# Downward products five units behind the upward ones instead of four

## The chip, the core and the metric

The kernel runs on one core of one Trainium2 chip. The metric is the device time of one execution in microseconds (us), lower is better. The engines go by the profile's names: PE is TensorE's matmul stream and PEld its weight loads, DVE is VectorE, ACT ScalarE, POOL GpSimd, and SP is SyncE, which here only issues DMAs.

## What is computed

Four batches of 12608 tokens with 128 channels go through an attention with 32 inducing points, and its output through a channel mix with a hidden width of 1024:

```python
h = mab(I, x)                  # 32 inducing points attend to all tokens
x = mab(x, h)                  # every token attends to the 32 results
xk = mu_k * x + (1 - mu_k) * x_prev      # x_prev: the token before
xr = mu_r * x + (1 - mu_r) * x_prev
k = np.maximum(xk @ w_k, 0.0)            # 128 -> 1024, "upward"
v = k * k @ w_v                          # 1024 -> 128, "downward"
r = 1.0 / (1.0 + np.exp(-(xr @ w_r)))    # the gate
out = r * v
```

## The kernel before

Each batch is cut into 25 groups of 512 tokens (the last has 320), and each group into four units of 256 of the 1024 hidden channels, so there are 100 units in a batch and 400 in all. A table `units` lists them, and one loop runs over them with the step number `n`; `u` is the place of the unit in its group, 0 to 3. The schedule is written out by hand: every engine carries out its instructions in the order in which this loop emits them, and waits by semaphores for what they need.

Step `n` emits, in this order:

- `gate` (L816, DVE), in the step after a group's last downward product: the output in the PSUM bank `ps_v` times the gate `rT`.
- `up(n)` (L780, L782, PE): four matmuls of 512 columns into one of two `ps_a` tiles. They read `R`, the attention's weights of this group's tokens, and `W`, the hidden layer's weights folded with the inducing points' values.
- `square(n)`: DVE takes the maximum with zero out of `ps_a` into `k_t` (L792; called relu below). ACT squares it into `kh`, rounded to the matmul's format (L797), and into `k_t` (L798). POOL forms the rest `kl`, the difference of the two (L800). In two steps of twelve (`high_vector`) DVE makes `kh` instead of ACT (L794), and ACT's L798 then waits for it.
- `zgate` (L769, L770 on PE; L772 on ACT) in one step of four, `u == 1`: two matmuls into the group's `ps_v` bank and the sigmoid from there to `rT`. The downward products later write over the same bank, so the first of them waits for the sigmoid.
- `store` (L827, DVE; L834, SP), one step after `gate`: a transpose, and after every second group four DMAs of 128 KB to the output.
- `down(n - LAG)` (L811, PE): six matmuls, `kh` by two weight tiles and `kl` by one.
- the `events` of step `n`: the attention of later tokens, cut into small pieces with a step number each.

Of these events three matter here. `stage_a` prepares the next batch: `btr` (L331, DVE, then four DMAs `xt<-xs`, L334) transposes tokens at steps s-1, s, s+1 and s+3 of each twelve, through three `xs` buffers. `stage_b` makes `R`: its softmax pieces run on DVE and ACT, its last DVE piece is `al` (L661), and `spread` (L594, L671) one step later issues five DMAs a group on SP, one of them the halo of one column from the group before, for four groups in four steps. SP issues its DMAs strictly in the emitted order.

`kh` and `kl` have as many buffers as the distance `LAG`, so `kh` of unit n goes where that of unit n - LAG was, and waits for the downward product that step n emits. `k_t` has four buffers, `ps_a` and `ps_v` two each.

Before the loop a head reads batch 0, runs its first attention and converts the weights; it borrows the buffers of `kh` and `kl` (`halves`).

Of the kernel before, what the change touches and what calls it, by code (L numbers as in the profile page):

```python
# [8 lines left out]
F32 = mybir.dt.float32  # L9
F32R = mybir.dt.float32r  # L10
# [9 lines left out]
def kernel(  # L20
# [11 lines left out]
    nc = tc.nc  # L32
# [3 lines left out]
    P = 128  # L36
    Q = 4
    FC = F // P
    G = 512
# [2 lines left out]
    TAIL = N - (NBLK - 1) * BLK  # L42
    WF = F + C
    UC = 2
    LAG = 4
    UO = 2
    NU = FC // UC
    assert NBLK == 7 and C == P and M * Q == P and F % 1024 == 0 and TAIL % Q == 0
# [9 lines left out]
    mp = ctx.enter_context(tc.tile_pool(name="mp", bufs=2))  # L58
# [530 lines left out]
    def halo(S, g, far=True):  # L589

        if g == 0:
            nc.vector.memset(S.R[g].bitcast(F32)[:, 0:1], 0.0)
        elif far:
            nc.sync.dma_start(out=S.R[g].bitcast(F32)[:, 0:1], in_=S.R[g - 1].bitcast(F32)[:, G:G + 1])  # L594
        else:
            nc.vector.tensor_copy(out=S.R[g][:, 0:1], in_=S.R[g - 1].bitcast(F32)[:, G:G + 1])
# [157 lines left out]
    class Group:  # L754
# [31 lines left out]
        def square(self, u, on_vector):  # L786

            w = self.w
            k = mp.tile([P, UC * G], F32, name="k_t", bufs=4).rearrange("p (c t) -> p c t", c=UC)[:, :, :w]
            kh = mp.tile([P, UC, G], F32R, name="kh", bufs=4)[:, :, :w]  # L790
            kl = mp.tile([P, UC, G], F32R, name="kl", bufs=4)[:, :, :w]
            nc.vector.tensor_scalar(out=k, in0=self.ps[:, :, :w], scalar1=0.0, scalar2=None, op0=ALU.max)  # L792
            if on_vector:
                nc.vector.scalar_tensor_tensor(out=kh, in0=self.ps[:, :, :w], scalar=0.0, in1=k,  # L794
                                               op0=ALU.max, op1=ALU.mult)
            else:
                nc.scalar.activation(out=kh, in_=k, func=AF.Square)  # L797
            nc.scalar.activation(out=k, in_=k, func=AF.Square)  # L798
            self.h[u] = (kh, kl)
            return lambda eng, a, z: eng.tensor_tensor(out=kl[:, :, a:z], in0=k[:, :, a:z],  # L800
                                                       in1=kh.bitcast(F32)[:, :, a:z], op=ALU.subtract)
# [36 lines left out]
    def run(th):  # L838
        for f in th:
            f()  # L840
# [6 lines left out]
    def halves():  # L847

        for name in ("kh", "kl"):
            for _ in range(4):  # L850
                yield mp.tile([P, UC, G], F32, name=name, bufs=4)

    pairs = halves()

    conv = {}
# [43 lines left out]
    def head():  # L899


        last = NBLK - 1
        for k in range(2):
            ab[k].tr()
        place(PARTS_FIRST)
        ab[0].scores()
        for k in range(NBLK):
            ab[k].maxi()
            ab[k].expo()
            place(PARTS[k][0])  # L910
            if k > 0:
                ab[k - 1].hmm()
            if k == last:
                maxes()
            if k > 0:
                ab[k - 1].acc()
            if k == 0:
                constants()
            if k + 2 < NBLK:
                ab[k + 2].tr()  # L920
            place(PARTS[k][1])
            ab[k].etrans()
            ab[k].ecopy()
            ab[k].sums()
            if k < last:
                ab[k + 1].scores()
            place(PARTS[k][2])
        spin(8)
        weights()
        ab[last].hmm()  # L930
        ab[last].acc()
        load_x(1, 0)
        hfin()
        assert not work
# [11 lines left out]
    def start():  # L946

        sc0, df0, ex0, nm0, pl0 = stage_b_head([0, 1])
        sc1, df1, ex1, nm1, pl1 = stage_b_head([2, 3])
        hi0, lo0, put0 = pl0[0]  # L950
        box = {}

        def bank():
            return pv.tile([P, G], F32, name="ps_v")

        def gate_bank(s):
            if s == 0:
                box["g"] = bank()
            return box["g"][:, s * C:(s + 1) * C]

        wa = [wpart(s, 0, bank) for s in range(2)]
        wb = [wpart(s, 1, bank) for s in range(2)]
        wg = [wpart(s, None, lambda s=s: gate_bank(s)) for s in range(2)]
        assert F // G == 2
        hi1, lo1, put1 = pl0[1]
        run([sc0, lambda: halo(batches[0], 0), df0, wa[0][0], wa[1][0], wa[0][1], ex0, wa[1][1], wa[0][2], nm0, wb[0][0], hi0, lo0, put0,
             wa[1][2], wb[0][1], hi1, lo1, wb[0][2]])
        for f in (wb[1][0], wb[1][1]):
            soon(0, f)
        for n, f in ((0, wb[1][2]), (0, sc1), (1, df1), (1, ex1), (2, nm1)):  # L970
            at(n, f)
        for prod, high, low in wg:
            at(1, prod)
        for prod, high, low in wg:
            at(1, high)
            at(2, low)
        soon(2, put1)
        for k, (high, low, put) in enumerate(pl1):
            at(k + 2, high)
            at(k + 3, low)  # L980
            at(k + 5, put)
        at(4, lambda: units[0][0].zgate(first=True))
# [22 lines left out]
    with tc.manual_schedule():  # L1005
        head()
        start()
        for n in range(len(units) + LAG + 2):
            grp, u = units[n] if n < len(units) else (None, n % NU)
            old, ou = units[n - LAG] if LAG <= n < len(units) + LAG else (None, 0)  # L1010
            m = n - LAG - 1
            if 0 <= m < len(units) and units[m][1] == NU - 1:
                units[m][0].gate()
            if grp is None:
                run(late)
                late = []
            else:
                grp.up(u)
                run(early.pop(n, []))
                low = grp.square(u, n in high_vector)  # L1020
                run(late)
                late = []
                part = grp.w - (grp.w // 2 if n >= len(units) - 3 else 0)
                low(nc.gpsimd, 0, part)
                if part < grp.w:
                    late = [lambda low=low, a=part, z=grp.w: low(nc.vector, a, z)]
                if n == end:
                    run(late)
                    late = []
                if n >= NU and u == 1:  # L1030
                    grp.zgate()
                if u == NU - 2 and n + 2 < len(units):
                    nxt = units[n + 2][0]
                    if nxt.b == 0 and nxt.g < Q:
                        halo(nxt.S, nxt.g, far=False)
            if 1 <= m <= len(units) and units[m - 1][1] == NU - 1:
                units[m - 1][0].store()
            if old is not None:
                old.down(ou)
            run(events.pop(n, []))  # L1040
# [30 lines left out]
```

## Time and profile before

| | |
|---|---|
| median of 3 runs | 1141.57 us (1140.73 to 1146.31) |
| profiled execution, first to last instruction | 1141.9 us |
| its own time | not given apart; its span is 0.3 us above the median |
| busy PE, PEld | 1100.8, 836.7 us |
| busy DVE, ACT, POOL | 917.5, 971.6, 948.5 us |
| POOL `kl` (L800), 400 times | 2.377 us each |
| DVE relu (L792), 400 times | 1.201 us each |
| ACT squares (L797, L798) | 1.040 and 1.049 us each |
| the loop's first upward product | at 58.26 us |

PE's busy time counts overlapped matmuls with modelled ends, so a short pause hides in it; the waits that the profile puts down to a releaser are the better guide. Idle time of another engine costs nothing unless PE waits for it in the end.

### The profile page before, as it was taken

What the parts mean: (1) busy time and instruction counts of PE and PEld (TensorE: products, weight loads), DVE (VectorE), ACT (ScalarE), POOL (GpSimd) and SP (SyncE); (2) the same over time, 40 slices, a digit from 0 to 9 for tenths busy, and PEclk for the clock granted to TensorE, in tenths of its full rate; (3) what the DMA queues carried; (4) which work ended last, traced back from release to release, by engine and by line L of the source; (5) the groups of instructions that cost most, each with busy time, mean ns of one, the idle gap of its engine ahead of it and who ended that gap; (6) DMA issues with size and microseconds to landing.
All of it is one profiled execution on the core that took longest, in us unless ns stands there. A gap on an engine that the chain in (4) does not pass through costs nothing.

```text
span 1141.9 us, 17672 instructions
## 1 busy us (share of the span) xinstructions
PE 1100.8 (96%) x5710; PEld 836.7 (73%) x5710; DVE 917.5 (80%) x1294; ACT 971.6 (85%) x1107; POOL 948.5 (83%) x413
## 2 busy tenths in 40 slices
PE   6788999999989999999999999999999999999997
PEld 4466777777777777777777777777778777777886
DVE  4787899887678988887777889898777888887665
ACT  4487888888988888888987988889889988889996
POOL 1157888988877988888889888888888899999996
PEclk9989999999999999999999999999999999999999
DMA  9213454555135455555134455545222233242212
GB/s 268 75 29 92 106 111 108 127 129 106 33 67 119 94 124 123 125 120 124 23 63 86 110 127 121 131 96 125 49 51 60 45 65 59 54 74 56 43 28 34
DMA packets 274988, 102.32 MB, mean 90 GB/s; under 512 B 234288, under 2 KB 249808, under 8 KB 272592
## 3 DMA queue, kind: packets, MB, share of 16 engines
q1 hardware_dynamic: 274560, 101.18, 40.8%
q8 instruction: 45, 0.74, 0.3%
q14 instruction: 47, 0.39, 0.1%
q10 hardware_dynamic: 336, 0.02, 0.0%
HBM read 28.07 MB, written 25.82 MB: 47 GB/s over the span
## 4 chain that ended last, share of the span: by engine, by line
PE 80%; DVE 9%; ACT 7%; issue 3%; DMA 1%; SPq 0%; DVEq 0%; ACTq 0%
PE ps_v L811 40%; PE ps_a L780 15%; PE ps_a L782 13%; DVE k_t L792 3%; PE pb_b L617 2%; PE ps_v L769 2%; PE ps_v L770 2%; PE pb_a L359 2%; PE pb_a L428 2%; ACT kh L797 2%; ACT L772 1%; ACT L634 1%; ACT k_t L798 1%; DVE kh L794 1%; PE ps_a L227 1%
## 5 line engine op out<-in xcount | busy, mean ns | idle before, releaser
L800 POOL TENSOR_TENSOR kl<-k_t,kh 128x1024 fp32r<-128x1024 f32 (+2 forms) x400 | 939.6, 2377 | 151.7 <-ACT k_t L798 131.2
L792 DVE TENSOR_SCALAR k_t<-ps_a 128x1024 f32<-128x1024 f32 (+1 forms) x400 | 480.4, 1201 | 153.9 <-PE ps_a L782 144.2
L798 ACT ACTIVATE k_t<-k_t 128x1024 f32<-128x1024 f32 (+1 forms) x400 | 418.6, 1049 | 38.6 <-DVE kh L794 22.2
L797 ACT ACTIVATE kh<-k_t 128x1024 fp32r<-128x1024 f32 (+1 forms) x352 | 366.1, 1040 | 89.5 <-PE ps_v L811 49.8
L780 PE MATMUL ps_a<-R,W 128*128 128x512 f32 (+1 forms) x800 | 325.2, 407 | 8.8 <-DMA R<-al 4.7
L782 PE MATMUL ps_a<-R,W 128*128 128x512 f32 (+1 forms) x800 | 314.7, 394 | 0.0
L811 PE MATMUL ps_v<-kh,wvh 128*128 128x512 f32 (+1 forms) x800 | 250.2, 394 | 5.3 <-ACT rT L772 4.7
L811 PE MATMUL ps_v<-kl,wvh 128*128 128x512 f32 (+1 forms) x800 | 249.1, 392 | 0.2 <-POOL kl L800 0.2
L811 PE MATMUL ps_v<-kh,wvl 128*128 128x512 f32 (+1 forms) x800 | 249.2, 392 | 0.0
L780 PEld LDWEIGHTS ps_a<-R,W 128*128 128x128 f32 x800 | 151.7, 190 | 82.9 <-issue 20.0
L811 PEld LDWEIGHTS ps_v<-kh,wvh 128*128 128x128 f32 x800 | 149.7, 189 | 44.0 <-ACT rT L772 9.9
L811 PEld LDWEIGHTS ps_v<-kl,wvh 128*128 128x128 f32 x800 | 150.3, 189 | 34.8 <-POOL kl L800 0.4
L811 PEld LDWEIGHTS ps_v<-kh,wvl 128*128 128x128 f32 x800 | 150.6, 189 | 34.2
L782 PEld LDWEIGHTS ps_a<-R,W 128*128 128x128 f32 x800 | 151.7, 190 | 30.8
L816 DVE TENSOR_TENSOR oT<-ps_v,rT 128x512 f32<-128x512 f32 (+1 forms) x100 | 66.7, 667 | 2.3
L827 DVE STREAM_TRANSPOSE ot<-oT 128x512 f32<-128x512 f32 x96 | 67.3, 701 | 0.0
L794 DVE SCALAR_TENSOR_TENSOR kh<-ps_a,k_t 128x1024 fp32r<-128x1024 f32 x48 | 58.8, 1225 | 5.4 <-DVE k_t L792 0.5
L772 ACT ACTIVATE rT<-ps_v 128x512 f32<-128x512 f32 (+1 forms) x99 | 57.3, 579 | 0.3
L331 DVE STREAM_TRANSPOSE xs<-xb 128x512 f32<-128x512 f32 x72 | 50.0, 695 | 3.6 <-DMA xt<-xs 1.8
L769 PE MATMUL ps_v<-R,W 128*128 128x512 f32 (+1 forms) x99 | 39.1, 395 | 1.4 <-DVE oT L816 1.4
L772 ACT ACT_TABLE_LOAD x31 | 39.8, 1283 | 0.5
L770 PE MATMUL ps_v<-R,W 128*128 128x512 f32 (+1 forms) x99 | 38.7, 391 | 0.0
(192 smaller groups left out, 609.5 us busy)
## 6 DMA issues: line engine op xcount, KB each, us to landing
out_dram<-ot SPq DMA_DIRECT2D x184, 128.0 KB, 3.3
xb<-in_x_dram SPq DMA_DIRECT2D x18, 1024.0 KB, 5.5
xt<-xs SPq DMA_DIRECT2D x288, 64.0 KB, 2.0
R<-ah SPq DMA_DIRECT2D x184, 64.0 KB, 2.0
R<-al SPq DMA_DIRECT2D x184, 64.0 KB, 2.0
kh<-in_x_dram SPq DMA_DIRECT2D x4, 512.0 KB, 7.9
kl<-in_x_dram SPq DMA_DIRECT2D x4, 512.0 KB, 7.5
xb<-in_x_dram SPq DMA_DIRECT2D x8, 256.0 KB, 5.3
```

What stands on the lines that cost most here:

```text
L769: nc.tensor.matmul(out=ps[:, :w], lhsT=S.W[0][:, F:WF], rhs=R[:, 1:w + 1], start=True, stop=False)
L772: nc.scalar.activation(out=self.rT, in_=ps[:, :w], func=AF.Sigmoid)
L780: nc.tensor.matmul(out=ps[:, c, :w], lhsT=S.W[0][:, cs], rhs=R[:, 1:w + 1], start=True, stop=False)
L782: nc.tensor.matmul(out=ps[:, c, :w], lhsT=S.W[1][:, cs], rhs=R[:, 0:w], start=False, stop=True)
L792: nc.vector.tensor_scalar(out=k, in0=self.ps[:, :, :w], scalar1=0.0, scalar2=None, op0=ALU.max)
L794: nc.vector.scalar_tensor_tensor(out=kh, in0=self.ps[:, :, :w], scalar=0.0, in1=k, op0=ALU.max, op1=ALU.mult)
L797: nc.scalar.activation(out=kh, in_=k, func=AF.Square)
L798: nc.scalar.activation(out=k, in_=k, func=AF.Square)
L800: return lambda eng, a, z: eng.tensor_tensor(out=kl[:, :, a:z], in0=k[:, :, a:z], in1=kh.bitcast(F32)[:, :, a:z], op=ALU.subtract)
L811: nc.tensor.matmul(out=self.v, lhsT=wt[:, fc, :], rhs=kk[:, c, :], start=(fc == 0 and n == 0), stop=(fc == FC - 1 and n == 2))
L816: nc.vector.tensor_tensor(out=self.oT, in0=self.v, in1=self.rT, op=ALU.mult)
L827: nc.vector.transpose(out=ot[:, o:o + w], in_=self.oT)
```

## The change

The distance becomes five units, with five buffers each for `kh` and `kl`. Since a group then ends one step later, `gate` and `store` move by themselves from `u` = 0 and 1 to `u` = 1 and 2 (they are emitted by the distance), and `zgate` is moved from `u == 1` to `u == 2` by its condition. The events keep their step numbers. The two additional buffers take 8 KB of each partition, and an argument of the program's set-up gives up part of the memory that is reserved there for DMA descriptors.

```diff
-    LAG = 4
+    LAG = 5
...
-            kh = mp.tile([P, UC, G], F32R, name="kh", bufs=4)[:, :, :w]
-            kl = mp.tile([P, UC, G], F32R, name="kl", bufs=4)[:, :, :w]
+            kh = mp.tile([P, UC, G], F32R, name="kh", bufs=LAG)[:, :, :w]
+            kl = mp.tile([P, UC, G], F32R, name="kl", bufs=LAG)[:, :, :w]
...
-                yield mp.tile([P, UC, G], F32, name=name, bufs=4)
+                yield mp.tile([P, UC, G], F32, name=name, bufs=LAG)
...
-                if n >= NU and u == 1:
+                if n >= NU and u == LAG % NU + 1:
                     grp.zgate()
...
-    nc = _bacc.Bacc("TRN2", target_bir_lowering=False, num_devices=1)
+    nc = _bacc.Bacc("TRN2", target_bir_lowering=False, num_devices=1,
+                     dynamic_dma_scratch_size=1024)
```

What this does to the order is shown at three places. The numbers behind names tell tiles apart, and they differ between the two programs.

On PE, at the loop's start, the rows from the end of `up(4)` on. Before:

```order
L782 MATMUL ps_a_861<-R_721,W1_710 128x512
L811 MATMUL ps_v_873<-kh_767,wvh_111 128x512 x2
L811 MATMUL ps_v_873<-kh_767,wvl_112 128x512 x2
L811 MATMUL ps_v_873<-kl_768,wvh_111 128x512 x2
L769 MATMUL pb_a_887<-R_716,W0_709 128x512
L770 MATMUL pb_a_887<-R_716,W1_710 128x512
L780 MATMUL ps_a_892<-R_721,W0_709 128x512
```

Now:

```order
L782 MATMUL ps_a_861<-R_721,W1_710 128x512
L769 MATMUL pb_a_880<-R_716,W0_709 128x512
L770 MATMUL pb_a_880<-R_716,W1_710 128x512
L780 MATMUL ps_a_885<-R_721,W0_709 128x512
L782 MATMUL ps_a_885<-R_721,W1_710 128x512
```

The first downward product stands behind `up(5)` now, and step 4 has none.

On DVE, steps 12 to 14, with a `high_vector` step first. Before:

```order
L816 TENSOR_TENSOR oT_1074<-ps_v_904,rT_907 128x512
L792 TENSOR_SCALAR k_t_1081<-ps_a_1076 128x1024
L794 SCALAR_TENSOR_TENSOR kh_1082<-ps_a_1076,k_t_1081 128x1024
L792 TENSOR_SCALAR k_t_1103<-ps_a_1098 128x1024
L827 STREAM_TRANSPOSE ot_1023<-oT_1074 128x512
L362 TENSOR_REDUCE mx1_1131<-pb_a_1126 128x1
L792 TENSOR_SCALAR k_t_1138<-ps_a_1133 128x1024
L371 TENSOR_SCALAR mh_1151<-mx1_1131 64x1
L377 TENSOR_SCALAR mkr_1153<-mh_1151 32x1
L661 TENSOR_TENSOR al_1155<-pb_b_921,ah_1096 128x512
```

Now:

```order
L792 TENSOR_SCALAR k_t_1073<-ps_a_1068 128x1024
L794 SCALAR_TENSOR_TENSOR kh_1074<-ps_a_1068,k_t_1073 128x1024
L816 TENSOR_TENSOR oT_1090<-ps_v_933,rT_936 128x512
L792 TENSOR_SCALAR k_t_1097<-ps_a_1092 128x1024
L362 TENSOR_REDUCE mx1_1115<-pb_a_1110 128x1
L792 TENSOR_SCALAR k_t_1122<-ps_a_1117 128x1024
L827 STREAM_TRANSPOSE ot_1036<-oT_1090 128x512
L371 TENSOR_SCALAR mh_1145<-mx1_1115 64x1
L377 TENSOR_SCALAR mkr_1147<-mh_1145 32x1
L661 TENSOR_TENSOR al_1149<-pb_b_910,ah_1088 128x512
```

`gate` has left the place ahead of `kh`, and the store's transpose (L827) stands behind the relu of step 14, one place ahead of `al`. The same stands at steps 193 to 195. The four output DMAs of these two stores come on SP directly ahead of the five of `spread`, both before and now.

On ACT, at steps 104 to 106, near the start of batch 1. Before:

```order
L798 ACTIVATE k_t_3790<-k_t_3790 128x1024
L634 ACT_TABLE_LOAD
L634 ACTIVATE s2_3755<-s2_3755 128x512
L797 ACTIVATE kh_3810<-k_t_3809 128x1024
L798 ACTIVATE k_t_3809<-k_t_3809 128x1024
L772 ACT_TABLE_LOAD
L772 ACTIVATE rT_3819<-ps_v_3816 128x512
```

Now:

```order
L798 ACTIVATE k_t_3782<-k_t_3782 128x1024
L634 ACT_TABLE_LOAD
L634 ACTIVATE s2_3749<-s2_3749 128x512
L797 ACTIVATE kh_3804<-k_t_3803 128x1024
L798 ACTIVATE k_t_3803<-k_t_3803 128x1024
L797 ACTIVATE kh_3822<-k_t_3821 128x1024
L798 ACTIVATE k_t_3821<-k_t_3821 128x1024
L772 ACT_TABLE_LOAD
L772 ACTIVATE rT_3831<-ps_v_3828 128x512
```

Two squares more stand ahead of the sigmoid (L772) now; the number of table loads is the same.

## The prediction

> **What bounds the kernel now.** First the page's totals, then PE's waits, then the rate in stretches without a wait. "Unit n" is a row of the table of units, and up(n), relu(n) and down(n) are its pieces.
>
> ```profile
> span 1141.9 us, 17672 instructions
> PE 1100.8 (96%) x5710; PEld 836.7 (73%) x5710; DVE 917.5 (80%) x1294; ACT 971.6 (85%) x1107; POOL 948.5 (83%) x413
> ```
>
> PE is busy for 96% of the span, and no other engine comes above 85%. Two stretches of twelve units each show the rate (columns: stretch, length, then busy time of PE, PEld, DVE, ACT and POOL, granted clock, DMA share, GB/s):
>
> ```profile
> 203.50:236.46 32.96, 32.96 (x178) 24.59 (x175) 29.80 (x42) 28.78 (x33) 28.75 (x13) 1.00 0.51 122
> 947.75:978.73 30.98, 30.84 (x139) 23.69 (x135) 25.25 (x29) 27.63 (x30) 28.58 (x13) 1.00 0.30 58
> ```
>
> PE is filled in both, at a full clock, and the others have 3 us or more to spare in 33. A unit takes 2.75 us here and 2.58 us in the last batch. What PE waits for, out of the list of its waits (us in total, times, longest):
>
> ```profile
> PE ps_a L780 <- DMA R<-al: 4.7, 2, 2.4
> PE ps_v L811 <- ACT rT L772: 4.7, 5, 1.2
> PE ps_a L780 <- ACT R L745: 3.6, 2, 2.9
> PE ps_v L769 <- DVE oT L816: 1.4, 1, 1.4
> ...
> PE ps_v L811 <- POOL kl L800: 0.2, 1, 0.2
> ```
>
> The last row is the one that a longer distance would shorten: the downward products waited 0.2 us in all for POOL's `kl`. A fifth unit of distance buys time that nobody lacks. What the change can do to the time lies in the start, the end, and the few places above where a moved `gate`, `store` or `zgate` meets something late.
>
> In the regular stretches a moved DVE piece is covered. The tightest pair of rows there is the relu of unit 141 and the upward product that needs its bank:
>
> ```profile
> 453.89 1.22 DVE L792 TENSOR_SCALAR k_t<-ps_a 128x1024 f32<-128x1024 f32 x1
> 456.94 0.40 PE L780 MATMUL ps_a<-R,W 128*128 128x512 f32 x1
> ```
>
> The relu ends at 455.11, 1.83 us before PE comes to up(143). The largest piece that moves ahead of any relu is 0.70 us (the transpose, a row below), which leaves 1.1 us. I cost the regular segments at nothing; without that cover each of the 24 could lose up to 0.7 us.
>
> **The change, part by part.**
>
> *Start and end.* The first downward product moves from step 4 to step 5, so PE does one less while it waits for others anyway, and one more after the last upward product.
>
> ```profile
> 67.67 0.80 PE L780 MATMUL ps_a<-R,W 128*128 128x512 f32 x1 [2.87 <-ACT R L745]
> 77.76 0.66 PE L743 MATMUL pb_a<-ident,ah 128*128 128x128 f32 x4 [0.50 <-ACT rT L772]
> 350.94 0.63 PE L811 MATMUL ps_v<-kh,wvh 128*128 128x512 f32 x2
> 352.33 0.40 PE L780 MATMUL ps_a<-R,W 128*128 128x512 f32 x1
> ```
>
> At 77.76 PE waits for the first sigmoid, a chain through DVE and ACT that does not get shorter when PE has less to do: the down and the `zgate` that are missing by then become idle time. Six matmuls of a downward product take 352.33 - 350.94 = 1.39 us, so +1.4 us. (Zero at the least, if PE were the bound there; the wait says it is not.) At the end:
>
> ```profile
> 1133.90 0.46 PE L811 MATMUL ps_v<-kh,wvh 128*128 128x320 f32 x2
> 1134.20 0.46 PE L811 MATMUL ps_v<-kh,wvl 128*128 128x320 f32 x2
> 1134.84 0.55 PE L811 MATMUL ps_v<-kl,wvh 128*128 128x320 f32 x2 [0.18 <-POOL kl L800]
> ```
>
> A pair takes 0.30 us (1133.90 to 1134.20), the last one came 0.64 after its forerunner: 0.34 us were lost to `kl`. With 1.4 us more work ahead of it this wait is gone: -0.3 us.
>
> *Unit 16, where `R` comes late.*
>
> ```profile
> 98.92 0.70 DVE L827 STREAM_TRANSPOSE ot<-oT 128x512 f32<-128x512 f32 x1
> 99.65 2.63 SPq L834 DMA_DIRECT2D out_dram<-ot  x4
> 101.72 1.22 DVE L792 TENSOR_SCALAR k_t<-ps_a 128x1024 f32<-128x1024 f32 x1 [0.40 <-PE ps_a L782]
> 102.38 0.90 SPq L594 DMA_DIRECT2D R<-R  x1
> 105.47 0.58 SPq L671 DMA_DIRECT2D R<-al  x1
> 107.74 0.68 PE L780 MATMUL ps_a<-R,W 128*128 128x512 f32 x1 [2.39 <-DMA R<-al]
> ```
>
> The store (98.92) moves behind relu(14) (101.72). Its four output DMAs keep SP for 2.63 us and stand ahead of `spread`. The relu starts where its own up lets it, and can end at 101.6 if DVE has nothing else in front; the transpose then ends at 102.3, the outputs at 105.0, and five DMAs of about 0.58 follow, the last issued near 107.35 instead of 105.47: +1.9 us. If the relu ends as it does now (102.94) it is +3.2 us. If SP's line is no limit, what is left is the 0.70 us by which `al` comes later behind the transpose. I take +1.9, since `zgate` no longer stands ahead of up(14) on PE and the relu can start earlier.
>
> *Unit 100, the other late `R`.* No output DMA stands there (the group is even), only the transpose ahead of `al`:
>
> ```profile
> 335.17 0.69 DVE L661 TENSOR_TENSOR al<-pb_b,ah 128x512 fp32r<-128x512 f32 x1 [0.48 <-ACT ah L657]
> ```
>
> Of its 0.70 us 0.48 fit into this idle time: +0.2 us (between 0 and 0.7).
>
> *The sigmoid.* Five times a group's first down waits for it. At unit 108:
>
> ```profile
> 352.39 0.48 DVE L816 TENSOR_TENSOR oT<-ps_v,rT 128x320 f32<-128x320 f32 x1
> 354.11 1.23 DVE L794 SCALAR_TENSOR_TENSOR kh<-ps_a,k_t 128x1024 fp32r<-128x1024 f32 x1
> 355.43 1.06 ACT L798 ACTIVATE k_t<-k_t 128x1024 f32<-128x1024 f32 x1 [1.91 <-DVE kh L794]
> 362.44 0.73 PE L811 MATMUL ps_v<-kh,wvh 128*128 128x512 f32 x2 [1.21 <-ACT rT L772]
> ```
>
> From 355.43 on ACT runs without a pause to that sigmoid. `gate` (352.39) no longer stands ahead of `kh`, so ACT starts 0.48 us earlier. The sigmoid moves behind one more unit's two squares, 2.1 us at 1.06 each, while PE has one more step of at least 2.3 us (1.39 for a down and four sixths of it for an up): another 0.2. Of 1.21 us about 0.5 stay: -0.7 us, and the same at unit 308. The waits at units 12 and 96 stand ahead of the late `R` of 16 and 100, so what they give comes back there: 0. With no relief it is 0 at each, with full relief -1.2.
>
> *Units 204 to 206.* Here SP runs late, and DVE waits for it:
>
> ```profile
> 598.08 2.69 SPq L834 DMA_DIRECT2D out_dram<-ot  x4
> 600.87 0.83 SPq L671 DMA_DIRECT2D R<-ah  x1
> 603.27 0.58 SPq L671 DMA_DIRECT2D R<-al  x1
> 605.27 0.51 SPq L594 DMA_DIRECT2D R<-R  x1
> ...
> 618.71 5.23 SPq L334 DMA_DIRECT2D xt<-xs  x8
> ```
>
> ```profile
> 597.35 0.70 DVE L827 STREAM_TRANSPOSE ot<-oT 128x512 f32<-128x512 f32 x1
> 599.03 1.23 DVE L792 TENSOR_SCALAR k_t<-ps_a 128x1024 f32<-128x1024 f32 x1 [0.97 <-PE ps_a L782]
> ...
> 622.75 0.71 DVE L331 STREAM_TRANSPOSE xs<-xb 128x512 f32<-128x512 f32 x1 [1.80 <-DMA xt<-xs]
> 626.96 0.50 PE L780 MATMUL ps_a<-R,W 128*128 128x512 f32 x1 [0.34 <-DVE kh L794]
> ```
>
> From 600.87 to 618.71 SP's line is a chain: each group's halo (605.27) waits until the group before has landed. At its end `btr` of step 203 waits for the DMAs of an earlier `btr` (1.80 us), and behind it on DVE stand `gate`, relu(204) and its `kh`, for which PE waits in `zgate` (the 1.4 of the list) and up(206). The store at 597.35 moves behind relu(194), to 600.26; its outputs then begin at 601.0 and end at 603.7, and the last DMA of the first `spread` is issued at about 605.55 instead of 603.27. These 2.3 us pass down the chain, `btr` starts at 625.0, `kh` ends near 628.75 (`gate` no longer ahead of it), and PE is at up(207) 2.2 us later than before, after 5 us of idle time: +2.2 us. If the chain has slack that I don't see, it is 0; if nothing is made good, 2.9.
>
> *The clock there.* After the two idle times of 2.4 us the granted clock is halved:
>
> ```profile
> 107.80:111.20 3.40, 3.40 (x9) 2.64 (x9) 1.40 (x2) 0.00 (x0) 3.40 (x2) 0.50 0.35 77
> 339.90:343.30 3.40, 3.40 (x12) 2.99 (x11) 1.84 (x2) 0.74 (x1) 2.30 (x2) 0.51 0.30 64
> ```
>
> 3.4 us at half rate are 1.7 us lost. An idle time of 5 us at unit 206 should bring a third such stretch: +1.7 us (0 to 3.4), and at half rate PE comes to the down of unit 208 after the sigmoid, so the wait of 1.2 us there goes: -1.2. At units 16 and 100 the stretch is there already: 0.
>
> The Trainium skill (TensorE: Matmul & The Clock Gate, Part 1) says that the clock falls to half after at least one idle window of some 3.4 us. Idle times of 2.39 and 2.34 us, less than a window, were enough here, so page and trace differ, and the rows decide; by the page too 5 us would do, but with the store's DMAs hidden, and about 2.7 us of idle time at unit 206, the page's rule would add nothing and the rows' rule 1.7 us.
>
> *Free.* The two buffers cost no instruction, table loads keep their number, and no DMA is issued by POOL, so I cost the smaller reserve for descriptors at 0; if it throttled SP's DMAs, it would show at units 16, 100 and 206, some tenths at each.
>
> **Sum:** 1.4 - 0.3 + 1.9 + 0.2 - 0.7 - 0.7 + 2.2 + 1.7 - 1.2 = +4.5 us. On the span of 1141.9 this is 1146.4, on the median, 0.3 lower, 1146.
>
> **Rivals.**
>
> *SP's line has slack, and only start, end and sigmoid are left:* 1.4 - 0.3 + 0.2 - 0.7 x 3 = -0.8, about 1141. For it: every late piece is 20 us or more upstream of the wait, and DVE's order shifts too. Against it: the rows of SP above follow each other without a gap. 26%.
>
> *Slower by over 0.5%, by the idle time at unit 16 and the clock:* `spread` at unit 16 comes at its latest (+3.2 instead of 1.9), and PE's longer idle time there brings one more stretch of 3.4 us at half clock (+1.7): 1146 + 3.0 = 1149. For it: the clock fell after much shorter idle times. Against it: relu(14) waits 0.40 us for PE, so it can start earlier. It decides once the last DMA of `R` for unit 16 is issued after 108.5. 18%.
>
> *Faster:* the pieces fall so that `R` comes in time. Without the waits for `R` (-4.7), their two half-clock stretches (-3.4) and two of the sigmoid's (-1.4), with start and end (+1.1): 1133. Against it: the store moves towards `al` and `spread` at both, never away. 6%.
>
> *The change does nothing but start and end,* +1.1, 1142.7, is in the first rival's reach.
>
> **How the numbers follow.** A measurement here tells about 0.5% (5.7 us) from no change. My case takes the remaining 50% at 1146 +- 3, a quarter of it over 1147.3. Slower by over 0.5%: 0.5 / 4 + 0.18, about 0.3; faster 0.06; within 0.64. The range reaches from the first rival less what two full sigmoid reliefs would give (1140) to the slow rival with the sigmoid's waits not relieved (1149 + 1.4).
>
> **What would show it.** In the profile after: PE's wait for `R<-al` at its first place near 4 to 5 us instead of 2.39; the output DMAs of 99.65 at 102 or later; DVE's wait at step 203 near 4 us, a PE wait of some 5 us for `kh` (L794), and a half-clock stretch after it; waits for the sigmoid below 3 us in all; none for `kl`; the last upward product about 3 us later than now, and 1.4 us more behind it. I am wrong if SP's chain before unit 204 takes up the delay, or if regular segments of twelve take more than 32.96 us.

## The result, and the profile after

The changed kernel takes 1162.12 us (median of 4 runs, 1158.16 to 1164.27) and the kernel before 1142.2 us (1140.73 to 1146.31): a ratio of 1.0162, 95% interval 1.0135 to 1.0189. That is +19.9 us where +4.5 was predicted. The profiled execution after took 1158.16 us, the shortest of the four, and its span is 13.2 us longer than that of before; what the other three lost beyond that stands in no trace. One execution of those below, in run 6, was a slow one (1208.75 us at a mean granted clock of 0.849); it is in that run's median and in no ratio. The page of the profiled execution opens with

```profile
span 1155.1 us, 18041 instructions
PE 1108.6 (96%) x5710; PEld 837.9 (73%) x5710; DVE 918.0 (79%) x1294; ACT 972.5 (84%) x1107; POOL 947.7 (82%) x413
```

The busy time of VectorE, ScalarE and GpSimd moved by less than 1 us; PE's rose by 7.8, a part of it at half clock. From PE's list of waits (total, times, longest), against the rows of the prediction:

```profile
PE ps_a L780 <- DMA R<-al: 5.9, 1, 5.9
PE ps_a L780 <- DVE kh L794: 4.6, 3, 3.6
...
PE pb_a L339 <- ACT e1t L396: 2.4, 2, 1.3
PE ps_a L780 <- DMA xt<-xs: 2.4, 1, 2.4
PE pb_a L743 <- ACT rT L772: 1.9, 1, 1.9
PE ps_v L811 <- ACT rT L772: 1.6, 3, 0.6
```

The wait for `kl` is gone. The waits for the sigmoid went from 4.7 to 1.6 us. The late `R` of unit 16 grew from 2.39 to 5.87 us, and at unit 206 stands the predicted wait for `kh`. The waits for `e1t`, at units 165 and 265, are new. The one that the profile puts down to `xt` is the late `R` of unit 100 (2.34 us before): an upward product reads `R` and `W`, and no `xt`. Units 16 and 206 have a half-clock stretch behind them (table of stretches, with the columns of the prediction's first such table; the clock is the third figure from the end):

```profile
106.10:112.90 6.80, 3.58 (x9) 2.83 (x10) 1.43 (x2) 0.00 (x0) 3.23 (x2) 0.52 0.39 89
635.10:638.50 3.40, 3.40 (x11) 2.64 (x10) 3.30 (x5) 3.37 (x4) 2.38 (x1) 0.55 0.80 127
```

These were in the sum. What was not is in the stretch of twelve units that the prediction showed at 32.96 us (units 50 to 62):

```profile
204.82:239.42 34.60, 34.60 (x178) 24.96 (x174) 29.91 (x43) 30.29 (x34) 30.34 (x14) 1.00 0.56 123
```

1.64 us more, at a full clock, and PE counts as busy throughout. The one piece of PE's work that grew by more than 0.12 us is stage A's `scores` (L359), whose eight matmuls took 1.07 us before and 2.66 after (PE before, then after):

```profile
235.47 1.07 PE L359 MATMUL pb_a<-xt,indT 128*32 128x512 f32 x8
```

```profile
236.84 2.66 PE L359 MATMUL pb_a<-xt,indT 128*32 128x512 f32 x8
```

They wait for `xt`, and SP (after) shows why it comes late: the last four `xt` DMAs stand behind the output DMAs and a spread.

```profile
202.20 3.05 SPq L834 DMA_DIRECT2D out_dram<-ot  x4
205.34 0.74 SPq L204 DMA_DIRECT2D xb<-in_x_dram  x1
...
227.67 3.06 SPq L834 DMA_DIRECT2D out_dram<-ot  x4
...
234.49 2.43 SPq L334 DMA_DIRECT2D xt<-xs  x4
```

Before, the load of `xb` (L204) was issued 1.82 us ahead of unit 50 (203.50); now it comes 0.52 us behind the start of unit 50 (204.82). Before:

```profile
201.68 0.95 SPq L204 DMA_DIRECT2D xb<-in_x_dram  x1
```

`btr` waits for it on VectorE (after):

```profile
212.44 0.71 DVE L331 STREAM_TRANSPOSE xs<-xb 128x512 f32<-128x512 f32 x1 [1.50 <-DMA xb<-in_x_dram]
```

SP sends what `btr` makes. It idles from 211.06 until 213.18, when the segment's first `xt` can go, and from there its line is filled up to the last. That first `xt` came 6.15 us behind the start of unit 50 before (at 209.65) and comes 8.36 us behind it now.

SP's line as a whole is late, and the place where it became late is one segment earlier. SP before, around unit 38:

```profile
165.44 2.43 SPq L334 DMA_DIRECT2D xt<-xs  x4
167.97 0.53 SPq L204 DMA_DIRECT2D xb<-in_x_dram  x1
170.16 3.74 SPq L834 DMA_DIRECT2D out_dram<-ot  x4
173.94 1.41 SPq L594 DMA_DIRECT2D R<-R  x1
175.45 0.54 SPq L671 DMA_DIRECT2D R<-ah  x1
```

and VectorE there:

```profile
169.42 0.70 DVE L827 STREAM_TRANSPOSE ot<-oT 128x512 f32<-128x512 f32 x1
173.67 0.69 DVE L661 TENSOR_TENSOR al<-pb_b,ah 128x512 fp32r<-128x512 f32 x1
```

SP has one free stretch in a segment: behind the load of `xb` there is nothing in its line but these outputs until the next spread, whose `al` is still to be made. Before, the transpose ended at 170.12, the outputs were issued at 170.16, and they lay in that free stretch: they ended at 173.90, `al` at 174.36. After:

```profile
166.78 2.43 SPq L334 DMA_DIRECT2D xt<-xs  x4
169.32 0.53 SPq L204 DMA_DIRECT2D xb<-in_x_dram  x1
175.05 2.63 SPq L834 DMA_DIRECT2D out_dram<-ot  x4
177.73 1.03 SPq L594 DMA_DIRECT2D R<-R  x1
```

```profile
174.32 0.70 DVE L827 STREAM_TRANSPOSE ot<-oT 128x512 f32<-128x512 f32 x1
175.60 0.69 DVE L661 TENSOR_TENSOR al<-pb_b,ah 128x512 fp32r<-128x512 f32 x1
```

The transpose stands one step later, right ahead of `al`. SP's order is the same, but SP now idles from 169.85 to 175.05, and then issues outputs until 177.68, ahead of a spread whose last source, `al`, is made by 176.29. The spread's first DMA is 1.37 us ahead of unit 40 before (175.31 less 173.94) and 0.64 us behind it now (177.73, unit 40 starts at 177.09): 2.0 us late. A store with outputs meets `al` like this at steps 14, 38 and 62 of batch 0, and at the like steps of the others: eleven times, nine of them inside a batch and two, at steps 194 and 294, ahead of the next batch.

### The profile page after: what moved, and what is told of

It is laid out like the page before. It is cut to its first block, busy times and chain, and to the rows that moved or that the text cites. A ratio compares the mean times of both kernels' runs of the same rounds, so it can differ in the third digit from the quotient of the medians.

```text
span 1155.1 us, 18041 instructions
## 1 busy us (share of the span) xinstructions
PE 1108.6 (96%) x5710; PEld 837.9 (73%) x5710; DVE 918.0 (79%) x1294; ACT 972.5 (84%) x1107; POOL 947.7 (82%) x413
## 4 chain that ended last, share of the span: by engine, by line
PE 77%; ACT 7%; DVE 6%; issue 3%; SPq 3%; DMA 2%; POOL 1%; ACTq 0%; DVEq 0%; POOLq 0%
PE ps_v L811 40%; PE ps_a L780 14%; PE ps_a L782 13%; ACT kh L797 3%; DVE k_t L792 2%; PE pb_a L359 2%; PE pb_b L617 2%; PE ps_v L769 2%; PE ps_v L770 2%; ACT k_t L798 2%; PE pb_a L428 1%; SPq L93 1%; SPq L190 1%; ACT L772 1%; POOL kl L800 1%
## 5 line engine op out<-in xcount | busy, mean ns | idle before, releaser
L827 DVE STREAM_TRANSPOSE ot<-oT 128x512 f32<-128x512 f32 x96 | 67.2, 700 | 0.0
L772 ACT ACTIVATE rT<-ps_v 128x512 f32<-128x512 f32 (+1 forms) x99 | 57.3, 579 | 0.3
```

Of the source, the lines that this page charges most:

```text
L772: nc.scalar.activation(out=self.rT, in_=ps[:, :w], func=AF.Sigmoid)
L827: nc.vector.transpose(out=ot[:, o:o + w], in_=self.oT)
```

## The experiments

Eighteen kernels, each timed against the kernel before on the same chip. Times are medians, ratios are to the kernel before, with 95% intervals.

**1. Outputs later, in the changed kernel.** `send` issues the four DMAs of a store.

```
-                units[m - 1][0].store()
+                sends[n + 3] = units[m - 1][0].store()
+            if sends.get(n):
+                sends[n]()
```

> The changed kernel, with only the store's four output DMAs issued three steps later (SP's line meets them at the same distance from the loads of stage A as before the change; transposes, gate and products stay where the change put them). Theory 'SP's line' (the loss of about 20 us comes from the output DMAs, which stand one step later ahead of spread and xt on SP): 1143 to 1150 us. Theory 'VectorE's order' (gate and transpose, one step later, stand ahead of al, xs and relu on VectorE): 1157 to 1164 us. Theory 'distance and buffers' (fifth unit, fifth buffers, smaller reserve for descriptors): 1157 to 1164 us.

1145.45 us, 1.0019 (1.0005 to 1.0034). Distance, buffers, gate and transposes are those of the changed kernel, and all but some 3 us of its loss are gone. The loss passes through the output DMAs.

**2. Outputs later, in the kernel before** (`n + 1` instead of `n + 3`, distance four).

> The kernel before (distance four), with only the four output DMAs of a store issued one step later, where the change issues them; the transpose stays in place. 'SP's line': 1154 to 1162 us. 'VectorE's order' and 'distance and buffers': 1140 to 1145 us.

1142.11 us, 1.0 (0.998 to 1.0019): nothing. "SP's line", as a matter of position alone, is refuted.

**3. Gate, store and `zgate` one step later, distance four.**

```
-            m = n - LAG - 1
+            m = n - LAG - 1 - 1
...
-                if n >= NU and u == 1:
+                if n >= NU and u == 2:
```

> The kernel before (distance four, four buffers), with gate, store and zgate one step later, as in the change. 'SP's line' and 'VectorE's order': 1155 to 1164 us. 'Distance and buffers': 1140 to 1146 us.

1197.4 us, 1.0468 (1.0433 to 1.0503). More than any theory said, since this kernel has a loss of its own. With the first down still at a distance of four, `zgate` one step later leaves the sigmoid no time, as PE's waits say:

```profile
PE ps_v L811 <- ACT rT L772: 27.5, 25, 2.7
```

So it tells little of the change, in which the down moves along.

**4. Buffers and reserve alone, nothing moved** (five buffers for `kh` and `kl`, `dynamic_dma_scratch_size=1024`).

> The kernel before (distance four), with five buffers for kh and kl and the smaller reserve for descriptors, and nothing moved. 'SP's line' and 'VectorE's order': 1140 to 1145 us. 'Distance and buffers': 1150 us or more.

1142.68 us, 1.0004 (0.999 to 1.0017). Both are free, as predicted.

**5. Outputs one step later, in the changed kernel.**

> The changed kernel, with the output DMAs issued one step later still; everything else in place. Theory 'wait' (SP takes its DMAs strictly in order, and stands at the outputs until the transpose of the same step is done, with spread and xt behind them): the transpose is done by then, 1143 to 1148 us. Theory 'place' (four output DMAs ahead of the last xt of a segment take SP's time, ready or not): 1157 to 1165 us, since they now stand right ahead of that xt. Theory 'VectorE's order' (the transpose ahead of al, xs and relu) for what is left: 1148 to 1157 us.

1159.03 us, 1.0136 (1.01 to 1.0172). "Place" seemed to win. The trace says otherwise: at the meeting with `al` SP has nothing between the two steps, so the move changed no order there, and SP still waits for the transpose (VectorE, then SP, of this run):

```profile
175.50 0.70 DVE L827 STREAM_TRANSPOSE ot<-oT 128x512 f32<-128x512 f32 x1
```

```profile
176.22 2.64 SPq L835 DMA_DIRECT2D out_dram<-ot  x4
```

My expectation was wrong about the kernel, not about the mechanism. For the same reason run 2 moved nothing at these places.

**6 and 7. The store, and the transpose alone, one step earlier, in the changed kernel.**

```
-            if 1 <= m <= len(units) and units[m - 1][1] == NU - 1:
-                units[m - 1][0].store()
+            k = m - 1 - -1
+            if 0 <= k < len(units) and units[k][1] == NU - 1:
+                units[k][0].store()
```

In run 7 the outputs stay where the change put them (`sends[n + 1]` takes what `store` returns, as in run 1).

> The changed kernel with the whole store (transpose and output DMAs) one step earlier, in the step of its gate, which is where it stood before; gate, zgate, distance and buffers as changed. 'Wait', 'place' and 'VectorE's order' all: 1142 to 1147 us. If the later gate or zgate costs more than that by itself: 1150 us or more.

> The changed kernel with the transpose alone one step earlier; SP's order is that of the changed kernel to the row, and only what the outputs wait for is done earlier. 'Wait': 1142 to 1147 us. 'Place': 1157 to 1164 us. 'VectorE's order': 1142 to 1147 us.

1144.18 us, 1.0016 (1.0001 to 1.0032), and 1145.47 us, 1.0022 (1.0009 to 1.0036). Run 7 has the changed kernel's order on SP, row for row, and is some 16 us faster. What costs is not where the outputs stand, but when their transpose is done.

**8. Only the store later, distance four, gate and `zgate` in place** (`k = m - 1 - 1`).

> The kernel before (distance four, gate and zgate in place), with the store (transpose and output DMAs) one step later. 'Wait': 1153 to 1162 us. 'Place': no more than the outputs alone one step later gave, 1140 to 1145 us. 'VectorE's order': 1145 to 1162 us. If the loss needs the longer distance: 1140 to 1145 us.

1170.96 us, 1.0243 (1.022 to 1.0266). The loss needs neither the distance nor the buffers. It is 9 us above what any theory said. In its trace PE waits 8.5 us in all for the sigmoid (4.7 before) and 10.0 us in `zgate` for `gate` (1.4 before); what each of them adds was not taken apart.

**9 and 10. Nine transposes.** `near` holds the steps two ahead of a segment's start. Of the stores that fall there, those with outputs go one step earlier (9), or all others do (10, `hit != (k == m)`).

```
+            near.add(s - 2)
...
+            for k in (m - 1, m):
+                if 0 <= k < len(units) and units[k][1] == NU - 1:
+                    hit = k + LAG + 2 in near and units[k][0].g % UO == UO - 1
+                    if hit == (k == m):
+                        units[k][0].store()
```

> The changed kernel with nine of its transposes one step earlier, and nothing else: those whose four outputs stand on SP ahead of a segment's first spread (two steps before the segment starts). SP's order and PE's are those of the changed kernel to the row. Theory 'gap' (SP has one idle time a segment, in which it waits for al; the outputs of every second segment lay in it, and now wait for their transpose until it is over, so spread, xt and the next xb load are issued some 3 us late): 1143 to 1149 us. Theory 'all stores a little' (each store that stands late costs its share, 9 of 100): 1158 to 1163 us.

> The other side: the changed kernel with all transposes one step earlier but those nine, which stay late. 'Gap': 1155 to 1163 us, nearly the whole loss with nine late transposes. 'All stores a little': 1143 to 1147 us.

1151.23 us, 1.0074 (1.0049 to 1.0098), and 1155.72 us, 1.0102 (1.0081 to 1.0123). Nine of 100 transposes carry more than half of the loss, from either side. Run 9 came out between the theories, run 10 at the lower end of 'gap'. In run 9's trace PE still waits 3.7 us for `kh` at unit 206: the store of step 194 is the same meeting, and was not among the nine.

**11 and 12. With step 194 and step 294, and the reverse** (`near.add(s + 22)` beside `combine`; run 12 is the kernel before with only these eleven one step later).

> The nine transposes of the run before, and the two at units 194 and 294 (the same meeting with al, at the start of a batch), one step earlier; the other 39 stores with outputs and all without stay late. 'Gap' at eleven places: 1143 to 1147 us. 'Gap' at nine places and something else for the rest: 1149 to 1153 us, as with nine.

> The kernel before (distance four, four buffers, gate and zgate in place) with these eleven stores one step later and nothing else. 'Gap': 1152 to 1168 us. If the loss needs the distance, the later gate, or the other stores: 1141 to 1147 us.

1148.23 us, 1.0048 (1.0033 to 1.0063), between its two ranges, and 1163.15 us, 1.0192 (1.0167 to 1.0218), as 'gap' has it. SP and VectorE around unit 38, in run 11:

```profile
168.25 3.47 SPq L834 DMA_DIRECT2D out_dram<-ot  x4
```

```profile
167.52 0.70 DVE L827 STREAM_TRANSPOSE ot<-oT 128x512 f32<-128x512 f32 x1
170.70 0.69 DVE L661 TENSOR_TENSOR al<-pb_b,ah 128x512 fp32r<-128x512 f32 x1
```

and in run 12:

```profile
176.46 2.63 SPq L834 DMA_DIRECT2D out_dram<-ot  x4
```

```profile
175.73 0.70 DVE L827 STREAM_TRANSPOSE ot<-oT 128x512 f32<-128x512 f32 x1
177.01 0.69 DVE L661 TENSOR_TENSOR al<-pb_b,ah 128x512 fp32r<-128x512 f32 x1
```

In run 11 the outputs are back in the free stretch, 13.9 of 19.9 us are back with them, and the longest wait for `kh` is 0.9 us. In run 12 eleven stores are one step late, in the kernel before, with nothing else of the change, and cost 21.0 us. That these eleven late stores make most of the loss is shown in both directions. That it is SP's wait for the transpose, and not the place of `al` behind it on VectorE, follows from run 1, which leaves every transpose ahead of `al` and loses only some 3 us.

**13 and 14. The other 6 us.** Run 13: early transposes in all groups behind which outputs stand (`hit = sends`). Run 14: the eleven, and all groups without outputs.

> The changed kernel with the transpose one step earlier in every second group, the ones behind which output DMAs stand (some 50); those of the other groups stay late. If what is left after eleven comes from waits of SP for transposes at the other outputs: 1142 to 1146 us. If it comes from the other groups' transposes on VectorE: 1147 to 1150 us, as with eleven.

> The eleven transposes and those of the groups without outputs one step earlier; the other 39 with outputs stay late. The reverse: 1147 to 1150 us if the rest comes from SP's waits at the other outputs, 1142 to 1146 us if from VectorE's order.

1144.89 us, 1.0009 (0.9997 to 1.002), and 1145.12 us, 1.002 (1.0009 to 1.0032). Both give most of it, so the runs do not put it down to the one or the other. Either relief being enough would fit a line with little slack; that is argued, not shown.

**15. The load of `xb` issued by ScalarE.**

```
-            nc.sync.dma_start(out=t, in_=x[b, j * BLK:(j + 1) * BLK, :].rearrange("(p s) c -> p s c", p=P))
+            nc.scalar.dma_start(out=t, in_=x[b, j * BLK:(j + 1) * BLK, :].rearrange("(p s) c -> p s c", p=P))
```

> The changed kernel with the loads of xb issued by ScalarE instead of SP, so that they no longer stand behind the late outputs. If the loss passes through the late load of xb (the transposes xs of the next segment wait for it): 1148 to 1156 us. If it passes through spread and xt alone: 1158 to 1163 us. If the issue on ScalarE costs ScalarE's line more than it gives: above 1163 us.

1223.14 us, 1.0702 (1.0678 to 1.0727): in the range of the third theory, but not by ScalarE's time. ScalarE issues the load, and SP's `xt` DMAs stand still until it has landed (the median from issue to landing of these loads is 5.0 us here):

```profile
169.67 0.33 ACTq L204 DMA_DIRECT2D xb<-in_x_dram  x1
```

```profile
165.78 0.59 SPq L671 DMA_DIRECT2D R<-al  x1
174.66 2.41 SPq L334 DMA_DIRECT2D xt<-xs  x4
```

What ties SP to that load is not in the trace, so this run does not tell how much of the loss passes through the late `xb`. The traces of the changed kernel and of run 12 tell more. After the loop's start `xb` is loaded seventeen times. In the changed kernel the first `btr` waits for the load at five of them, in the segments from units 52, 136, 160, 236 and 260: VectorE idles there for 0.84 to 2.11 us, and `btr` starts within 0.03 us of the landing. Before the change it did so at one, in that from unit 160 (1.27 us). In run 12 VectorE idles at the same five places, for 1.95 to 2.95 us, and again `btr` starts within 0.03 us of the landing; `gate` stands right behind `btr` there, and PE waits in `zgate` for `gate`, 0.57 to 1.58 us each time. So the late load is on the path at these five places in both kernels.

**16 to 18. Away from the late `R`.** Stage B of the first block of batches 1 to 3, and of the second block of batch 0, one step earlier, at a distance of four (16) and with run 6 (17); run 18 is run 16 with the outputs of step 13 issued five steps later.

```
-            stage_b(b, j + 1, at, s + 1)
+            stage_b(b, j + 1, at, s + 1 - (b == 0 and j == 0))
...
-            stage_b(b + 1, 0, at, s + 13)
+            stage_b(b + 1, 0, at, s + 12)
```

> The kernel before (distance four), with stage B of each batch's first block, and of the very second block, one step earlier, so that R is spread one step earlier ahead of units 16, 100, 200 and 300. If the two waits for R of 2.4 us and the two half-clock stretches of 1.7 us are on the path that sets the end: 1134 to 1139 us. If SP or VectorE gives the step back: 1141 to 1146 us.

> The changed kernel with the whole store in its gate's step and the same earlier stage B: distance five without the late transposes and without the waits for R. If these are independent: 1135 to 1140 us. If SP or VectorE gives the step back: 1143 to 1148 us.

> The kernel before (distance four) with the earlier stage B of the run d_early, and the very first store's outputs (step 13) issued five steps later, behind the first spread. If these outputs hold up R of unit 16 on SP: its wait of 2.4 us and the half-clock stretch go, 1135 to 1138 us. If VectorE or the chain from al sets R there: 1139 to 1141 us, as d_early.

1139.86 us, 0.9968 (0.9955 to 0.9981); 1142.16 us, 0.9999 (0.9988 to 1.0009); 1137.28 us, 0.9941 (0.9923 to 0.9958). Run 16 came out just above its first range, run 17 between its two; whether the gains of runs 6 and 16 add up cannot be told from intervals this wide. In run 16 the wait at unit 100 shrank to 0.9 us, and that at unit 16 stayed at 2.45: the first store's outputs still stood ahead of the spread. With them behind it, PE is filled there at a full clock (run 18):

```profile
90.00:110.00 20.00, 20.00 (x90) 15.06 (x89) 17.59 (x28) 17.09 (x19) 18.16 (x9) 1.00 0.24 75
```

Run 18 beats both kernels, the one before by 0.6%, at a distance of four.

## Why the prediction was wrong

*The step that failed* is "I cost the regular segments at nothing". It asked whether a moved piece on VectorE delays a relu and so the next upward product. That it does not was right: the list of PE's waits has one for a relu, 0.18 us at unit 5, and two of 0.80 and 0.20 us for a `kh` of VectorE at units 106 and 306 (the third is that of unit 206). It did not ask who else waits for the moved piece: SP does, for the transpose, with spread, `xt` and the load of `xb` behind it. The sum names just this for units 16 and 206, where the store moves behind relu(14) and relu(194), but takes these for the only places, where the same meeting recurs in every second segment. The prediction had said that it would be wrong if regular segments of twelve took more than 32.96 us; that was the sign that came. The price there is not paid where the meeting is, but a segment later: by the starts of the upward products, the twelve units from unit 40, where a meeting is, took 32.97 us before and 32.98 after, and the next twelve 32.94 and 34.58. Four other segments behind a meeting (from units 124, 148, 224, 248) grew by -0.03 to 0.16 us, the next ones (136, 160, 236, 260) by 0.94, 1.76, 1.13 and 2.96. These five lost 8.4 us in this execution: 5.7 us of it in `scores`, and most of the rest in the two waits for `e1t`. In run 12, where nothing else of the change was made, the same five grew by 1.69, 2.11, 2.07, 2.54 and 1.84 us. Not every meeting costs: those of steps 62, 294, 322 and 346 show no loss of their own in this trace; behind them no `btr` waits for a load. Runs 11 and 12 put the eleven meetings at 14 to 21 us, unit 16 and unit 206 among them.

Point by point, by the other steps:

- *Start, +1.4:* right. The wait for the first sigmoid went from 0.50 to 1.9 us.
- *End, -0.3:* the wait for `kl` is gone, right; up(396) is 12.7 us later and the end 13.2, so what stands behind it grew by 0.5 us, not by the 1.1 of the two terms. The additional product is not on the path that ends. The last outputs stand on SP behind those of the group before, whose `gate` stands on VectorE behind its half of unit 399's `kl`, and that piece waits for ScalarE. It starts 4.28 us after up(399) before and 4.79 us after it now.
- *Unit 16, +1.9 (0.7 to 3.2):* under-sized. The wait grew by 3.5 us, 1.2 of them because PE reaches it that much earlier (up(14) is 2.37 us earlier than before, up(8) 1.15). The half-clock stretch is twice as long, but 3.2 of its 6.8 us lie in the wait. Up(20) is 1.78 us later than before, where up(8) was 1.15 us earlier: +2.9, near the slow rival's +3.2.
- *Unit 100, +0.2:* 2.34 became 2.37 us, within its 0 to 0.7; the half-clock stretch behind it was not there this time (below).
- *Sigmoid, -0.7 at units 108 and 308:* right in kind; from unit 104 to 112 the kernel gained 0.45 us, from 304 to 312 0.42.
- *Units 204 to 206, +2.2, clock +1.7, sigmoid -1.2:* up(208) comes 2.67 us later against up(204), up(212) 1.45 earlier against that: +1.2 where +2.7 was forecast. The idle time on PE was 3.64 us instead of 5.
- *Buffers, reserve:* free (run 4).

Of the rivals the slow one had the right direction and the size at unit 16 about right, but it put its whole 3 us there and nothing in the segments. The one most readers would hold, that a longer distance must help, is answered by run 6: with the late transposes undone, distance five gives 1.0016, so it is worth nothing here.

## What to carry to other kernels

When a step is moved, follow not only the engine that runs it but each queue that waits for its result, and find the queue's idle time: work that fits into it is free, and the same work one step later can cost the idle time and its own length both. A place that was found to be tight is looked for again at its period, and its price may be paid a segment later, in rows that count as busy. Undoing the move for the suspected instances only, and making it for them only, settles such a case in two runs.

## What the hardware showed

Half-clock stretches lie on a grid. In every one of these executions their starts are whole multiples of 3.41 us apart, and each lasts a multiple of that. What decides in these traces is PE's idle time within one window of the grid, not the length of an idle time. Run 11 waited 3.63 us at unit 16, over two windows that hold 1.64 and 1.55 us of PE work, and kept its clock. Run 9 waited only 2.35 us at unit 100, most of it in one window with 1.41 us of work, and got the next one at half clock. Run 11, then run 9:

```profile
101.51:104.93 3.42, 1.64 (x8) 0.98 (x6) 2.38 (x5) 3.24 (x5) 3.42 (x3) 1.00 0.62 111
104.93:108.34 3.41, 1.55 (x7) 1.32 (x8) 0.28 (x1) 0.52 (x1) 3.41 (x2) 1.00 0.44 102
108.34:111.75 3.41, 3.41 (x19) 2.49 (x21) 3.41 (x5) 2.17 (x3) 0.84 (x2) 1.00 0.36 81
```

```profile
333.20:336.61 3.41, 1.41 (x7) 0.79 (x5) 1.57 (x4) 3.13 (x7) 3.41 (x3) 1.00 0.36 87
336.61:340.03 3.42, 3.07 (x7) 2.49 (x8) 0.91 (x1) 0.73 (x1) 2.62 (x2) 0.50 0.41 90
```

Over the profiles of both kernels and all 18 experiments, between 95 and 1110 us, 48 windows at full clock were followed by one at half: each had PE idle for 1.89 us or more (matmul ends as the profile models them). 5853 were not, and the most idle of these had 1.87 us. The Trainium skill (TensorE: Matmul & The Clock Gate, Part 1) says that the window runs freely, which these grids agree with, and that the clock falls after at least one idle window; here some 1.9 us of idle time in a window of 3.41 were enough. So a stretch behind a wait of 2.4 us, which the prediction counted as fixed, is there or not by where the wait falls on the grid: 1.7 us each. Each kernel has one trace, so that this changes between executions of one kernel is argued, not shown; the mean granted clock of the executions of the kernel before, 0.988 to 0.997, fits it.
